# A planned order of steps, reckoned with shorter landings of loads and searched anew

## The chip, the cores and the metric

One core of one Trainium2 chip runs the whole program. The metric is the device time of one execution in microseconds (us); a kernel's time is the median of its runs. TensorE is called PE here, VectorE DVE, ScalarE ACT, GpSimd POOL; SP is the queue that issues nearly all DMAs.

## The reference

Three layers follow one another, all in float32: an attention over 32 pooled memory slots (4 batches, 8 heads, 576 tokens, 64 wide), a gated layer and a layer with a leaky ReLU, both over the 2304 x 512 result.

```python
a = softmax(phi, axis=2)                       # over the 576 tokens, 32 slots
k_m = einsum('bhsm,bhsd->bhmd', a, k)          # pooled keys; v_m the same with v
attn = softmax(q @ k_m^T / 8) @ v_m
x = attn.transpose(0, 2, 1, 3).reshape(2304, 512)
x = ((x @ w_a) * (x @ w_b)) @ w_out            # 512 -> 1536 -> 512
h = x @ w_in                                   # 512 -> 2048
out = maximum(0.01 * h, h) @ w_out2            # 2048 -> 512
```

## The kernel before

The work has two stages. The first (up to 382 us of the profile) holds the attention, the gated layer and the preparation of the weights of the last layer; the second is the last layer, whose loops are written out by hand and which the change doesn't touch.

In the first stage nothing is ordered by hand. Functions such as `plan_att`, `plan_wab`, `plan_wo`, `plan_w`, `plan_ab`, `plan_x1` and `plan_pair` hand steps to a planner, the class `Plan` at the head of the file. A step has an engine, a cost in us, the steps that it needs, a due time, and a function that emits its instructions. `Plan.run` plays the engines forward in time: each engine takes, among the steps that could start first, the one with the smallest `latest`. `Plan.order` first sets `latest` from the due times and a few passes back and forth, then shifts it with `shifts`: each number in `SEEDS` draws one window of the plan and moves some of the steps in it by up to 12 us either way. The result is one order of steps for each engine's queue, and each queue is worked off in that order on the chip. So the planner's clock has no direct effect there: only the order that it leads to, and the number of filling matmuls, counts.

The filling matmuls (`warm`, line 1680) are products of constants that go into PE's queue wherever the planner reckons PE to be idle, as long as its clock is below `WARM` = 27.0 us. They are 512 or 256 columns wide and compute nothing that is used.

Loads and stores go through one queue in the planner. Each takes its own cost (0.85 us for a half of `phi`, 2.0 and 1.05 for the two parts of the first `k`, 2.5 and 1.05 for those of the first `v`, 1.5 for a half of `q`, 1.46 for a 512 KB weight block), from 0.8 us on. A load's data is reckoned to be there at the end of its cost plus a lag `late`. The lag begins at `LATE[0]` = 4.0. It is raised by `FETCHED` at the first load that is put in behind 9.0 us, raised again by `FETCHED`, up to `LATEST`, whenever PE's instructions enter a new block of 256 behind 20 us while the DMA queue is busy, and set to `LATE[1]` = 2.3 when the queue has stood idle for over 1 us:

```python
# lines 207-208, in issue(); lines 297-300, in run()
if free[DMA] + 2.0 > entered > 20.0:
    late[0] = min(late[0] + self.FETCHED, self.LATEST)
...
if at > free[DMA] + 1.0:
    late[0] = self.LATE[1]
elif free[DMA] > 9.0 and late[0] == self.LATE[0]:
    late[0] += self.FETCHED
```

The start of the plan matters for what follows. The first twelve loads have a fixed rank: the halves of `phi`, `k` and `q` of batch 0, the first two weight blocks (`wab` 0, of `w_a` and `w_b`), the two parts of `v`, two more weight blocks. A weight block is widened by three steps: the high words on ACT (line 438), the low words on POOL (line 446) or ACT (line 442), and their joining on DVE (line 456). From `v` a chain goes through PE, ACT and DVE: pooling (`km`, line 771), division (`kc`, line 844), transposition (`kvT`, line 858), the product with the weight block (`wp`, line 1183), its parts on ACT and DVE (`W`, lines 1208 and 1212). A second chain goes from `q` through the scores to the softmax on DVE (the last division is line 1100), the transposition of its result (`aT`, line 1110) and its parts (`AT`, lines 1123 and 1127). Both meet in the first `ab` product (line 1246), which needs `W` and `AT`. From there on the planner has real work for PE at all times: `ab`, the products with `w_out` (`x1p`, line 1312), the attention of batches 1 to 3, and the further `wp`.

Of the kernel before, what the change touches and what calls it, by code (L numbers as in the profile page):

```python
# [46 lines left out]
class Plan:  # L47
# [10 lines left out]
    BLOCK, FETCH, FETCH_ALONE, START = 256, 6.9, 4.8, 50.0  # L58
    CHANGE = 12
    SWITCH = {"rf": 0.1, "tf": 0.1, "fr": 0.28, "ft": 0.22, "rs": 0.1, "ts": 0.1, "sr": 0.3, "st": 0.23, "fs": 0.2, "sf": 0.2}  # L60
    LATE, FETCHED, LATEST = (4.0, 2.3), 1.2, 5.2
    SEEDS = (683652, 560159, 530175, 125177, 433488, 159828, 165231, 686446, 405802, 158260, 349165, 253408, 67255,
# [4 lines left out]
    PASSES, URGENT, WASTE = 30, 1.0, 0.3  # L67

    def __init__(self, **pools):
# [25 lines left out]
    def order(self, idle=None):  # L95
# [16 lines left out]
        for x, l in zip(self.steps, latest):  # L112
            x.latest = l
        for seed in self.SEEDS:
            for i, d in self.shifts(seed, best[2]):
# [1909 lines left out]
```

## Time and profile before

| What | us |
|---|---|
| Median of 3 runs (lowest to highest) | 738.47 (737.46 to 738.53) |
| The profiled execution | 738.45 |
| Its span, first to last instruction | 736.4 |
| PE busy / DVE busy / ACT busy in the span | 729.4 / 579.1 / 413.7 |
| Granted TensorE clock | 1.00 in the whole span |

The profile is of one execution. A row of a timeline begins with the start and the length of a piece in us; the engine, the line and the tiles that are written and read follow, with the number of instructions and, in brackets, the idle time of the engine before it and what ended that. The chain of work is followed back from the last instruction, at each step to what released it.

### The profile page before, as it was taken

The numbers are of one execution on the slowest core, as the hardware profiler recorded it, in microseconds if no ns is written. First come the engines' busy times: TensorE is split into PE (matmuls) and PEld (weight loads), VectorE is DVE, ScalarE is ACT, GpSimd is POOL, SyncE is SP. The second block draws the span as 40 slices with busy tenths as digits, with TensorE's granted clock in tenths as the row PEclk, the third lists the DMA queues.
The fourth block names the chain that finished last, engine by engine and source line by source line (L and its number), as shares of the span: only waits on it lengthen the run. The fifth ranks groups of instructions, "written<-read, shape, count | busy, mean of one in ns | idle before, by whom it ended". The sixth has DMA issues, their size and how long they took to land.

```text
span 736.4 us, 14535 instructions
## 1 busy us (share of the span) xinstructions
PE 729.4 (99%) x5391; PEld 654.2 (89%) x5391; DVE 579.1 (79%) x1196; ACT 413.7 (56%) x915; POOL 20.1 (3%) x38
## 2 busy tenths in 40 slices
PE   8999999999999999999999999999999999999997
PEld 5787887988889798888899999999999999999987
DVE  5987786967809999998746767998866997877797
ACT  3886684866729787856414455644444743454442
POOL 1210000001300000000000000000000000000000
PEclk9999999999999999999999999999999999999999
DMA  9995267474605989876527877778987777997493
GB/s 312 359 395 184 77 219 246 158 241 131 218 3 199 319 311 320 296 239 250 206 93 253 263 252 250 254 256 256 295 286 258 261 245 249 288 289 246 152 304 88
DMA packets 87495, 175.27 MB, mean 238 GB/s; under 512 B 7553, under 2 KB 36737, under 8 KB 87425
## 3 DMA queue, kind: packets, MB, share of 16 engines
q1 hardware_dynamic: 86736, 173.77, 70.6%
q8 instruction: 42, 0.69, 0.4%
q10 hardware_dynamic: 688, 0.59, 0.3%
q14 instruction: 29, 0.23, 0.1%
HBM read 140.25 MB, written 34.08 MB: 237 GB/s over the span
## 4 chain that ended last, share of the span: by engine, by line
PE 93%; DVE 3%; DMA 2%; ACT 1%; issue 0%; SPq 0%; DVEq 0%
PE h L1750 24%; PE x1p L1312 19%; PE ab L1246 19%; PE o L1850 15%; PE o L1854 8%; PE wp L1183 3%; DMA stage<-in_moe_w_b_dram 1%; PE sc L1050 1%; PE qT L1014 1%; PE km L758 1%; PE km L771 1%; PE aT L1110 1%; PE warm L1680 1%; DMA phi_t<-in_phi_dram 1%; DVE w2o L1434 0%; PE h L1825 0%
## 5 line engine op out<-in xcount | busy, mean ns | idle before, releaser
L1850 PE MATMUL o<-w2o,S 128*128 128x512 f32 (+1 forms) x504 | 177.1, 386 | 0.0
L1246 PEld LDWEIGHTS ab<-AT,W 128*128 128x128 f32 x1152 | 154.8, 188 | 7.0 <-ACT W L1208 2.5
L1246 PE MATMUL ab<-AT,W 128*128 128x288 f32 x1152 | 160.0, 297 | 0.2
L1312 PE MATMUL x1p<-G,wo 128*128 128x512 f32 (+1 forms) x720 | 156.5, 372 | 0.0
L1802 ACT ACTIVATE S<-g 128x384 fp32r<-128x384 f32 x168 | 87.6, 523 | 99.2 <-PE o L1850 85.9
L1312 PEld LDWEIGHTS x1p<-G,wo 128*128 128x128 f32 x720 | 123.5, 189 | 22.2 <-issue 0.8
L1750 PE MATMUL h<-T,ring 128*128 128x384 f32 x720 | 141.8, 335 | 0.0
L1854 PE MATMUL o<-w2o,S 128*128 128x256 f32 x492 | 137.6, 280 | 0.0
L1750 PEld LDWEIGHTS h<-T,ring 128*128 128x128 f32 x720 | 120.9, 188 | 4.1
L1803 DVE TENSOR_TENSOR S<-g,S 128x384 fp32r<-128x384 f32 x168 | 91.5, 553 | 40.4 <-ACT S L1802 40.2
L1850 PEld LDWEIGHTS o<-w2o,S 128*128 128x128 f32 x504 | 93.7, 188 | 14.5
L1854 PEld LDWEIGHTS o<-w2o,S 128*128 128x128 f32 x492 | 92.8, 189 | 0.0
L1872 DVE TENSOR_TENSOR C<-C,o 128x768 f32<-128x768 f32 x75 | 71.0, 949 | 13.9 <-ACT C L1876 7.9
L1750 PE MATMUL h<-B,ring 128*128 128x384 f32 x288 | 57.2, 336 | 0.0
L1793 DVE TENSOR_TENSOR g<-g 128x384 f32<-128x384 f32 x96 | 52.3, 552 | 2.9 <-ACT g L1760 2.4
L1750 PEld LDWEIGHTS h<-B,ring 128*128 128x128 f32 x288 | 48.8, 188 | 1.6
L438 ACT ACTIVATE stage<-stage 128x512 f32<-128x512 f32 x68 | 46.0, 686 | 5.6 <-DMA stage<-in_moe_w_in_dram 2.5
L1268 DVE TENSOR_TENSOR g<-a_sb,ab 128x288 f32<-128x288 f32 x96 | 42.1, 446 | 5.8 <-PE ab L1246 4.8
L1263 ACT COPY a_sb<-ab 128x288 f32<-128x288 f32 x96 | 38.3, 402 | 12.9 <-PE ab L1246 12.5
L1283 ACT ACTIVATE G<-g 128x576 fp32r<-128x576 f32 x48 | 33.2, 691 | 12.6 <-DVE g L1268 12.5
L1212 DVE TENSOR_TENSOR W<-wp,W 128x256 fp32r<-128x256 f32 (+1 forms) x75 | 35.1, 491 | 5.5 <-ACT W L1208 4.7
L1208 ACT ACTIVATE W<-wp 128x256 fp32r<-128x256 f32 (+1 forms) x75 | 30.3, 449 | 15.9 <-PE wp L1183 8.4
(143 smaller groups left out, 737.5 us busy)
## 6 DMA issues: line engine op xcount, KB each, us to landing
w2o<-a_scr SPq DMA_DIRECT2D x168, 256.0 KB, 3.8
ring<-a_scr SPq DMA_DIRECT2D x72, 512.0 KB, 4.4
stage<-in_moe_w_out_dram SPq DMA_DIRECT2D x28, 512.0 KB, 5.2
a_scr<-w2o SPq DMA_DIRECT2D x24, 512.0 KB, 3.7
a_scr<-a_out SPq DMA_DIRECT2D x24, 512.0 KB, 4.1
stage<-in_moe_w_in_dram SPq DMA_DIRECT2D x16, 512.0 KB, 5.2
stage<-in_moe_w_a_dram SPq DMA_DIRECT2D x12, 512.0 KB, 8.4
stage<-in_moe_w_b_dram SPq DMA_DIRECT2D x12, 512.0 KB, 7.5
```

The costliest lines, as they stand in the source:

```text
L438: act.activation(out=x, in_=x, func=ACTF.Prelu, scale=2.0 ** -112, alpha=2.0 ** 32)
L1246: pe.matmul(out=c[x, n][:, :HS], lhsT=W[b, f][:, hw, g, 128 * x:128 * x + 128], rhs=AT[b][:, g, ha, n * HS:(n + 1) * HS], start=(g == 0 an ...
L1263: act.copy(c["sb"][:, n], c[0, n][:, :HS])
L1268: dve.tensor_tensor(out=c["g"][:, n], in0=c["sb"][:, n], in1=c[1, n][:, :HS], op=ALU.mult)
L1312: pe.matmul(out=c["ps"], lhsT=wo_t[f][:, hw, 128 * m:128 * m + 128], rhs=G[f][:, hg, first:first + n], start=(f == fs[0] and (hw, hg) == P ...
L1750: pe.matmul(out=out, lhsT=ring[i % 2, part][:, o, kp, hw], rhs=x[:, hx], start=fresh and kp == 0 and (hw, hx) == PASSES[0], stop=kp == 1 a ...
L1793: dve.tensor_tensor(out=t, in0=x, in1=y, op=op)
L1802: act.activation(out=t[:, 0], in_=src, func=ACTF.Copy)
L1803: dve.tensor_tensor(out=t[:, 1], in0=src, in1=t[:, 0].bitcast(F32), op=ALU.subtract)
L1850: pe.matmul(out=dst[:, u, :y - x], lhsT=hi, rhs=wide[:, x:y], start=fresh and x == 0, stop=False, skip_group_check=True,)
L1854: pe.matmul(out=dst[:, u, :256], lhsT=lo, rhs=t[:, 0], start=False, stop=q == 3, skip_group_check=True,)
L1872: o_adds.append(lambda x=x: dve.tensor_tensor(out=total[name], in0=total[name], in1=x, op=ALU.add))
```

## The change

Two of the planner's constants are changed. The lag of a load is raised by 0.4 us instead of 1.2 us at a time, and to 4.8 us at most instead of 5.2. The list of seeds is a new one, of 105 numbers where there were 53. No step, cost or due time is different, so the same instructions run on the chip but for the number of filling matmuls; their order in the queues of the first stage is another one.

```diff
-    LATE, FETCHED, LATEST = (4.0, 2.3), 1.2, 5.2
-    SEEDS = (683652, 560159, 530175, 125177, 433488, 159828, 165231, 686446, 405802, 158260, 349165, 253408, 67255,
...
+    LATE, FETCHED, LATEST = (4.0, 2.3), 0.4, 4.8
+    SEEDS = (735747, 237875, 338390, 284576, 668393, 453202, 159564, 193473, 1221, 69595, 734897, 407191, 651114,
...
```

## Rows read from the trace of the kernel before

**Rows 1.** Stretches of the span: length, busy time of each engine, granted clock, DMA share, GB/s
```profile
0.00:27.09 27.09, 24.41 (x328) 16.26 (x328) 18.67 (x42) 11.75 (x24) 5.49 (x19) 1.00 0.99 324
27.09:60.00 32.91, 32.87 (x372) 28.39 (x365) 29.67 (x55) 28.33 (x55) 4.85 (x6) 1.00 0.95 346
60.00:382.33 322.33, 321.80 (x2662) 279.58 (x2661) 247.39 (x571) 210.02 (x502) 9.73 (x13) 1.00 0.61 210
382.33:736.40 354.07, 350.31 (x2041) 329.95 (x2039) 283.35 (x531) 163.59 (x336) 0.00 (x0) 1.00 0.77 247
```

**Rows 2.** Groups by line, PE up to 27.09 us: the filling matmuls
```profile
L1680 PE MATMUL warm<-const-float32-1.0 128*128 128x256 f32 (+1 forms) x22 | 10.0, 570 | 0.8 <-PEq L2009 0.8
```

**Rows 3.** Chain of work, 10 to 30 us: start, length, piece
```profile
18.72 0.09 PE sc L1056 x4
18.81 1.49 PE warm L1680 x4
20.30 2.17 PE km L771 x72
...
24.32 0.59 PE wp L1183 x16
24.92 1.13 PE aT L1110 x9
...
26.50 0.67 PE wp L1183 x16
27.17 3.13 PE ab L1246 x19
```

**Rows 4.** Timeline of SP, the tenth and the fifteenth load
```profile
8.06 2.24 SPq L570 DMA_DIRECT2D kv_t<-in_v_dram  x1
17.47 1.14 SPq L431 DMA_DIRECT2D stage<-in_moe_w_b_dram  x1
```

**Rows 5.** DMA issues, the same two: KB, us from issue to landing
```profile
kv_t<-in_v_dram SPq DMA_DIRECT2D x1, 384.0 KB, 10.5
stage<-in_moe_w_b_dram SPq DMA_DIRECT2D x1, 512.0 KB, 8.6
```

**Rows 6.** Timeline of ACT, the step behind the pooling of v
```profile
22.50 0.62 ACT L844 ACTIVATE kc<-km,r 128x128 f32<-128x128 f32 x2 [1.31 <-PE km L771]
```

**Rows 7.** Timeline of DVE, around the last division of the first softmax
```profile
23.38 0.76 DVE L1100 TENSOR_TENSOR s<-s,m 128x576 f32<-128x576 f32 x1
24.06 0.68 DVE L456 SCALAR_TENSOR_TENSOR wab<-stage 128x512 int32<-128x512 int32 x1
25.42 0.42 DVE L1212 TENSOR_TENSOR W<-wp,W 128x256 fp32r<-128x256 f32 x1 [0.68 <-ACT W L1208]
25.76 0.68 DVE L456 SCALAR_TENSOR_TENSOR wab<-stage 128x512 int32<-128x512 int32 x1
```

**Rows 8.** Stretch of 10 us, columns as in rows 1
```profile
40.00:50.00 10.00, 9.96 (x79) 8.23 (x78) 8.67 (x15) 8.08 (x18) 1.18 (x1) 1.00 1.05 396
```

**Rows 9.** Who waited for whom, PE from 27 to 345 us: us, times, longest
```profile
PE aT L1110 <- DVE s L1100: 0.2, 1, 0.2
PE kvT L926 <- ACT kmn L917: 0.2, 1, 0.2
```

**Rows 10.** Chain of work over the span: an early and a late run of ab
```profile
27.17 5.40 PE ab L1246 x36
...
338.04 19.32 PE ab L1246 x144
```

**Rows 11.** Timeline of SP, the first of five loads issued in a row
```profile
176.08 0.37 SPq L431 DMA_DIRECT2D stage<-in_moe_w_b_dram  x1
```

**Rows 12.** Chain of work, 176 to 196 us
```profile
178.49 8.90 DMA stage<-in_moe_w_b_dram
...
187.41 0.70 ACT stage L438
188.11 0.29 ACT a_sb L1263
```

12 rows, old and new, of the table SEEDS are left out of this document.

## The prediction

> **What bounds the kernel now.** I read the stretches of the span first [rows 1]. PE is busy for 32.87 of 32.91 us from 27.09 to 60, for 321.80 of 322.33 in the rest of the first stage, and for 350.31 of 354.07 in the second, whose code the change doesn't touch. So PE's queue sets the time, and an order of steps can win in three places only: in the first 27.09 us, in the 0.6 us of idle time of the first stage behind them, and in what is lost between matmuls that count as busy.
>
> In the first 27.09 us PE is busy for 24.41 us, but 10.0 of these are the 22 filling matmuls [rows 1, 2]. That is waiting under another name. What ends it is read from the chain of work [rows 3]: scores of batch 0 up to 18.81, then four fillers of 1.49 us, the pooling of `v` at 20.30, `wp` at 24.32, `aT` at 24.92, a second `wp`, and at 27.17 the first `ab`. PE works its queue off in order, so the pooling could not begin before the fillers ahead of it were through, even if its data was there.
>
> It was there. The second part of `v` was issued at 8.06 and landed 10.5 us later, at 18.56 [rows 4, 5]. The planner's own clock, summed from its costs, has that load's end at 0.8 + 2 x 0.85 + 2.0 + 1.05 + 2 x 1.5 + 2 x 1.46 + 2.5 + 1.05 = 15.02 us, and with the lag of 5.2 its data at 20.22. So the lag measured is 18.56 - 15.02 = 3.5 us, and the fillers stand where the planner believed the data to be still away. The fifteenth load tells the same: its end is five weight blocks later, at 22.32; it landed at 17.47 + 8.6 = 26.07, a lag of 3.75 [rows 4, 5].
>
> **The change part by part.** (1) The lag of the early loads. By the code the raise comes with the eighth load, the first that is put in behind 9.0 us. From there the reckoned lag falls from 5.2 to 4.4, and to 4.8 once PE's instructions have entered a new block behind 20 us, against 3.5 to 3.75 measured. The new figure is nearer to the chip and still on the safe side of it, by 0.7 to 1.3 us: no early step gets into a queue ahead of data that is later than reckoned.
>
> `v` is reckoned to be there 0.8 us earlier, at 19.42 in place of 20.22. Worth: of the 1.49 us of fillers about 0.8 go, and the pooling begins about 0.8 earlier. The most is 1.49, all of the fillers [rows 3]. What follows must move too. ACT, next in the chain, had been idle for 1.31 us waiting for the pooling, so it can take the division 0.8 earlier [rows 6]. The first `wp` moves from 24.32 to about 23.5. The softmax chain comes in beside it: its last division ends on DVE at 23.38 + 0.76 = 24.14, and `aT` began at 24.92 because PE was in `wp` (24.32 + 0.59) [rows 3, 7]. With `wp` through by 24.1, `aT` can begin at 24.15, 0.77 earlier. Both chains thus move by about the same, and the first `ab` by 0.75 to 0.8, to about 26.4. DVE has room for it: 0.68 us idle at 25.42, and two joins of 0.68 at 24.06 and 25.76 of which at least the second can stand behind the parts of `AT` [rows 7]. That makes 0.68 + 0.68 = 1.36 us, the most that this start can give. The least is 0, if the search leaves DVE in another order in which the softmax ends later. I take 0.8, the row of the fillers cut by the change of the reckoning.
>
> (2) The stretch from 27.09 to 60 us. A PE that is 0.8 us ahead asks for its weights 0.8 us earlier, and the loads can't come earlier: the DMA engines stand at a share of 1.05 in the ten us behind 40 [rows 8]. What hides that is the earliness just measured, 1.5 us for the fifteenth load (26.07 against 27.52). PE's idle time in this stretch is 0.04 us [rows 1], so no load was on its path. Cost 0; if the cover is gone, the whole 0.8 is given back.
>
> (3) The lag behind 60 us. Behind a gap in the queue it starts at 2.3 before and after, but is then raised by 0.4 and not 1.2. Here the reckoning was not too long. Five weight blocks were issued from 176.08 on; the fifth, issued at 178.49, landed 8.90 us later at 187.39 [rows 11, 12]. One gap lag of 2.3 and five costs of 1.46 from 176.08 give 185.7, so the chip was 1.7 us later. ACT took that block's high words at 187.41, at the moment of landing, and the copy `a_sb` stood behind them until 188.11, with `ab` waiting for it in the chain [rows 12]. Shorter raises put more such conversions too early into ACT's queue, ahead of copies that PE needs. What PE loses to all waits from 27 to 345 us now is 0.2 + 0.2 us of idle time [rows 9], and some gaps hidden in busy time. I take 0; from below -0.4 (both idle times gone), from above +0.6 (three more of 0.2).
>
> (4) The new seeds. They put the attention of batches 1 to 3 and the weight work at other places between the same matmuls. What can be had or lost is seen in `ab`: the first 36 of a run take 5.40 / 36 = 150 ns each, 144 in a late run 19.32 / 144 = 134 ns [rows 10], so 36 x 16 ns = 0.58 us went in waits that no idle time shows. A new order may take that away or bring it at another place: 0, from -0.6 to +0.6.
>
> The sum is -0.8 + 0 + 0 + 0, against the profiled execution of 738.45, which lies 0.02 us under the median: 737.65, say **737.6 us**. Single bounds add up to -1.36 - 0.4 - 0.6 = -2.4 and 0 + 0.6 + 0.6 = +1.2; together from 736.1 to 739.7.
>
> **The rivals.** *A larger gain.* The search also finds the rest of the start, 1.36, and about half of parts (3) and (4), 0.5: 736.6. For it speaks that PE has 10.0 us of fillers at the start; against it that DVE has only 1.36 us to give.
>
> *Nothing comes of it*, which is also the case in which the reckoning's 0.8 doesn't reach the chip: the loads from 27 to 60 us set the pace, PE gains 0.8 at the start and waits 0.8 behind it, at `ab` or `x1p`: 738.4. For it speaks the DMA share of 1.05 [rows 8]; against it the 0.04 us of idle time and the 1.5 us of earliness. [...]
>
> *Slower.* Of part (3): after 60 us conversions are queued on ACT ahead of loads that land later than reckoned, and PE stops for lack of `W` or free `ab` banks. The lag is shorter by up to 0.8 us after one raise, so a stop costs up to 0.8. The start's gain is used up at one such stop; four of them make 738.45 - 0.8 + 3.2 = 740.9. For it speaks the load that landed 1.7 us behind the reckoning; against it that this cost PE no idle time that the waits show, because PE itself was late too.
>
> **How the numbers follow.** About what a measurement can tell from no change is 0.2%, 1.48 us here: under 736.97 is faster, over 739.93 slower. Forecast 0.50, larger gain 0.25, nothing 0.17, slower 0.08. The larger gain lies mostly beyond the bound: 0.21 of it, and 0.03 of the forecast, make faster 0.24. Of slower 0.06 lies beyond. The same is 0.70. The range reaches to the larger gain and past the case of nothing, 736.2 to 739.1; it leaves out the ends of the bounds added up and stops of more than one.
>
> **What would show it.** Right: fewer fillers between the scores and the pooling of `v`, that pooling near 19.5, the first `ab` near 26.4, and `h`, the first product of the second stage, earlier by the same. Wrong in part (1): the pooling earlier but `ab` still near 27.1, with DVE without idle time before it. Wrong in part (2): idle time of PE from 27 to 60 us that a load or a join ended. Wrong in part (3): new idle time or slower `ab` runs behind 60 us, with ACT on line 438 at the moment of a landing just ahead. Wrong in all: a second stage that doesn't take the same time.

## The result and the profile after

The changed kernel takes 741.92 us (median of 5 runs, 740.85 to 743.55) against 738.47 for the kernel before in the same comparison: a ratio of 1.0051, with a 95% interval of 1.0036 to 1.0066. It is slower by about half a per cent, and the prediction of 737.6 (736.2 to 739.1) was wrong, in the sign too.

The profiled execution took 740.85 us, its span is 738.8. Line numbers are higher by 4 than before. Stretches of the span with the same four borders as in [rows 1], that is the first `ab`, 60 us, and the first `h` (columns as there):

```profile
0.00:26.07 26.07, 24.58 (x326) 16.02 (x327) 18.34 (x42) 12.54 (x26) 4.86 (x18) 1.00 0.97 318
26.07:60.00 33.93, 33.63 (x370) 29.13 (x368) 31.82 (x57) 27.78 (x54) 5.41 (x7) 1.00 0.96 350
60.00:384.70 324.70, 322.76 (x2658) 279.34 (x2658) 243.71 (x567) 213.33 (x506) 5.29 (x7) 1.00 0.60 208
384.70:738.80 354.10, 350.37 (x2041) 329.96 (x2039) 283.44 (x531) 163.58 (x336) 0.00 (x0) 1.00 0.77 247
```

The first `ab` comes at 26.07 and not at 27.09: 1.02 us were gained at the start. The second stage is the same, 354.10 against 354.07. Between them lie 33.93 + 324.70 = 358.63 us against 32.91 + 322.33 = 355.24: 3.39 us more. The sum -1.02 + 3.39 + 0.03 is the 2.4 us by which the span grew. PE's idle time (length less PE's busy time) in these two stretches grew from 0.57 to 2.24 us, which makes 1.67 of the 3.39; the rest, 1.7, is time that counts as busy.

The start in the chain of work of the kernel after (answers [rows 3]):

```profile
18.16 0.09 PE sc L1060 x4
18.25 1.06 PE warm L1684 x2
19.31 2.17 PE km L775 x72
```

The fillers between scores and the pooling of `v` took 1.06 us and not 1.49, and the pooling began at 19.31 and not at 20.30. Of these 0.99 us the fillers are thus 0.43; the other 0.56 come from the scores, which ended at 18.25 and not at 18.81.

Who waited for whom, PE from 26.07 to 384.7 us of the kernel after (us in total, times, longest; answers [rows 9]):

```profile
PE kvT L930 <- issue: 1.2, 1, 1.2
PE ab L1250 <- DVE g L1272: 0.4, 1, 0.4
PE wp L1187 <- DVE wab L460: 0.3, 1, 0.3
```

Three single waits, and the largest is one that the kernel before doesn't have at all: "issue", time in which PE waited for nothing that the profile shows. Timeline of PE around it, kernel after (start, length, piece, idle time before it):

```profile
154.04 2.25 PE L762 MATMUL km<-kv_t,phi_t 64*32 64x128 f32 x144
156.22 0.38 PE L898 MATMUL km<-ones,es 128*128 128x2 f32 x2
156.47 1.63 PE L1316 MATMUL x1p<-G,wo 128*128 128x512 f32 x6
159.32 0.43 PE L930 MATMUL kvT<-ident,kmn 128*128 128x128 f32 x2 [1.22 <-issue]
```

The pooling of batch 3 on line 762 sends 144 matmuls and 144 weight loads through PE in 2.25 us, six matmuls of `x1p` follow, and then PE stands still for 1.22 us ahead of `kvT`. The weight load of this `kvT` had been done at 158.17; only its matmul didn't come.

What did PE wait for? Packets of 16384 bytes on DMA queue 8, of the kind "instruction", number 42 in the span, against 10778 matmuls and weight loads of PE: one for 257 on average. Counting PE's instructions in blocks of 256, the planner's own figure, with the same offset in every kernel, PE enters block 12 at 154.32, inside that pooling, and block 13 at 159.32, the moment at which it goes on; 257 of the recorded ones start in between. The DMA queues in two windows in between, kernel after (packets, MB, share of 16 engines):

```profile
q1 hardware_dynamic: 618, 0.83, 99.8%
...
q1 hardware_dynamic: 109, 0.39, 97.0%
q8 instruction: 1, 0.02, 6.1%
```

The first line is 154.32 to 156.94, the other two are 156.94 to 157.93. For 2.62 us after the block was entered the DMA engines carried nothing but stores and loads; then came the one instruction packet, 1 us long, and 1.4 us later PE went on. In the kernel before the same block is entered at 150.97, the DMA engines carry a single packet of 3.0% up to 151.61, and PE's packet starts at 151.62: no pause. The pooling and the first `kvT` there, timeline of PE, kernel before:

```profile
150.58 2.25 PE L758 MATMUL km<-kv_t,phi_t 64*32 64x128 f32 x144
...
155.47 0.33 PE L926 MATMUL kvT<-ident,kmn 128*128 128x128 f32 x1 [0.17 <-ACT kmn L917]
```

### The profile page after: what moved, and what is told of

Same layout as the page of the kernel before. It is cut to its first block, busy times and chain, and to the rows that moved or that the text cites. A ratio compares the mean times of both kernels' runs of the same rounds, so it can differ in the third digit from the quotient of the medians.

```text
span 738.8 us, 14487 instructions
## 1 busy us (share of the span) xinstructions
PE 731.3 (99%) x5389; PEld 654.5 (89%) x5389; DVE 577.3 (78%) x1196; ACT 417.2 (56%) x921; POOL 15.6 (2%) x32
## 4 chain that ended last, share of the span: by engine, by line
PE 94%; DVE 3%; ACT 2%; issue 1%; DVEq 0%; ACTq 0%
PE h L1754 24%; PE ab L1250 19%; PE x1p L1316 19%; PE o L1854 15%; PE o L1858 8%; PE wp L1187 3%; PE warm L1684 1%; PE sc L1054 1%; PE qT L1018 1%; PE km L762 1%; PE km L775 1%; PE aT L1114 0%; ACT W L1212 0%; ACT stage L442 0%; PE h L1829 0%
## 5 line engine op out<-in xcount | busy, mean ns | idle before, releaser
L1291 DVE TENSOR_TENSOR G<-g,G 128x576 fp32r<-128x576 f32 x48 | 36.1, 752 | 3.3 <-ACT G L1287 2.5
```

## The experiments

**The same kernels again.** The changed kernel once more, and the kernel before once more.

> The changed kernel unaltered, looked at a second time. Its five timed runs lie between 740.85 and 743.55 us, those of before between 737.46 and 738.73, so something in it differs from execution to execution. Theory A (a fixed loss of the order): the same places lose time as in its first profile, first of all PE idle for 1.2 us ahead of a kvT matmul near 158 us, and the time is 740.9 to 742. Theory B (the landings of the early loads decide, since the order leaves them no room): the first ab product is later than the 26.07 us of the first profile by as much as the loads ahead of it landed later, and the rest of the spread is there, in the first 60 us.

> The kernel before, unaltered, looked at a second time. In its first profile the second part of v landed at 18.60 us; in the profiles of four other kernels with the same first ten loads it landed at 19.0 to 20.2. If the landing differs from execution to execution: it is later here, up to 20.2, and the pooling of v and the first ab stay at 20.3 and 27.1 all the same, because the fillers stand ahead of them.

After: 742.62 us, ratio 1.0055 (1.0036 to 1.0074); first `ab` at 26.92, 359.22 us from there to `h`, the pause at the same `kvT`, 1.4 us. Before: first `ab` at 27.95, 354.93 to `h`. So the loss between `ab` and `h` repeats (3.4 to 4.3), and so does the pause. The start doesn't stand where it stood: it moved by 0.85 us in both kernels with the landings of the loads, and the expectation that it stays at 27.1 was a miss. The difference at the start, 1.03 here, repeats.

**The start alone.** The kernel before without the fillers between scores and the pooling of `v`, then without all up to `wp` (23.0 in place of 19.2):

```diff
-        return sorted(self.trial(idle, seen)[0], key=lambda x: x.start)
+        own = set(self.steps)
+        out = self.trial(idle, seen)[0]
+        out = [x for x in out if x in own or not 17.0 < x.start < 19.2]
+        return sorted(out, key=lambda x: x.start)
```

> The order of the kernel before, without the one 512-wide and the one 256-wide filling matmul between the scores and the pooling of v (1.49 us in the chain of before); nothing else differs. It does part (1) of the prediction alone. If the start's gain is real and is carried to the end: pooling of v near 19 us instead of 20.3, first ab 0.7 to 1.0 us earlier than 27.1, time 737.5 to 737.9. If it is given back (loads, DVE): ab earlier but the second stage begins where it did, 738.4. If DVE holds the first ab: ab still at 27.1.

> The kernel before without any filling matmul that the plan has between 17 and 23 us, those between scores and pooling and those between pooling, kvT and wp. Leaving out the first group alone moved the first ab by 0.8 to 1.0 and the median by nothing. Theory (the start is worth what it moves, but is given back in part where the loads from 27 to 60 us set the pace): first ab 25.9 to 26.4, time 737.6 to 738.5 against about 738.5 to 739.4 of before on the same chip, ratio 0.998 to 1.000. Rival (the fillers hold the granted clock up): clock under 1.0 somewhere in the first 40 us, and slower by over 1 us.

First `ab` at 26.27 and 26.34, 354.9 and 355.7 us from there to `h`; 738.50 and 738.66 us, ratios 0.9999 (0.9989 to 1.0008) and 0.9999 (0.9990 to 1.0007). The profiled start moves as the prediction's part (1) says, and the median shows nothing of it: the 737.5 to 737.9 that was expected of the first didn't come, though a gain of up to 0.8 us stays within the interval. Without these fillers too the mean granted clock was 0.999 and 1.000. With the fillers up to `wp` gone, the softmax holds PE instead, and some of the gain is lost right behind the start (0.4 us by 46 us). No version tried here beats the kernel before.

**Is the pause the instruction stream?** The changed kernel with other work in front of the first pooling, so that every later instruction of PE stands elsewhere in its blocks: 54 tiny matmuls added (216 instructions), fillers cut narrower (112 more), or three fillers replaced by 57 tiny matmuls (216 more).

```diff
             step.emit()
+            if step not in own and 2.0 < step.start < 3.0:
+                for _ in range(54):
+                    pe.matmul(
+                        out=warm_ps[:32, :16], lhsT=unit[:64, :32], rhs=unit[:64, :16], start=True, stop=True
+                    )
```

> The changed kernel with 54 tiny filling matmuls (216 PE instructions) put in at the start, while PE waits for the first phi. Modulo 256 that moves every place in PE's instruction stream by 40 against the blocks in which it is fetched. Theory A (the 1.2 us ahead of kvT near 158 us is a wait for the next block of PE's instructions, which the pooling's 288 instructions had used up too fast): that idle time is gone or at another instruction, the time 0.8 to 1.4 us under the changed kernel's. Rival (a semaphore, ACT or a DMA holds that kvT): the idle time is there at the same instruction, the time the same.

> The changed kernel with its filling matmuls cut narrower at equal total width (the first three into 6 of 88 columns, the other 512-wide ones into 4 of 128, the 256-wide ones into 2 of 128): 112 more PE instructions ahead of the first ab, no more time. If the wait of 1.4 to 1.5 us ahead of kvT near 158 us is for the next block of PE's instructions: it goes, as it went with 216 instructions, and here nothing is paid at the start, so the time is 1.2 to 1.6 us under the changed kernel's 742.3, at 740.7 to 741.1. If the wait only moves to another instruction: 742.3.

> The changed kernel with its first three 512-wide filling matmuls (they end before 6 us) replaced by 57 tiny ones of about the same time in all. So every later instruction of PE stands 216 places further back in its stream, and no step, wait or order is different. Theory (the 1.4 us near 158 us are PE waiting for its next block of 256 instructions, because a block is entered during the pooling of batch 3, whose 288 instructions pass in 2.2 us): the pause at the line of kvT behind that pooling goes, first ab stays near 26.1 to 26.9, from the first ab to h about 356.7 in place of 358.5 to 359.2, and the time is 740.3 to 741.2, some 1.4 to 1.8 under the changed kernel. Rival (the pause comes from the order: ACT's kmn or a queue of PE that waits for a tile): it stays at 1.2 to 1.4, and the time stays at 741.9 to 742.6. A mixed outcome: the pause goes and another one comes at another block's edge, with the same sum.

The pause is gone in all three. All three were expected to be faster than the changed kernel; they took 744.74, 744.22 and 743.33 us and were slower, since the first `ab` came at 30.84, 29.91 and 29.50. The narrow matmuls took longer than reckoned (the 57 of the third 6.23 us, where the fillers that they replace take 5.13), and what followed them was slower too (in the first kernel the two 256-wide fillers behind them took 1.06 us and not the 0.60 of the changed kernel, and the mean granted clock of the span was 0.998 against 1.000; in the third, four fillers that take 1.92 us in the chain of the changed kernel took 3.08). From `ab` to `h` the three took 356.74, 357.79 and 358.28 us. From the first `ab` to `h` there are the same matmuls in the same order in these kernels, so they can be laid on each other: at the `kvT` of the pause the three gain 1.28 us on the kernel after, but the next matmul takes 0.13 of it back, and in the third kernel an `aT` that now waits for DVE another 0.17. Net, the pause costs about 1.1 us. The hope of 356.7 held for the first only; the others lose again at single `ab` matmuls elsewhere (0.65 us ahead of the one at 196.78 in the second, 0.3 ahead of the one at 271.44 in the third).

**Does the fetch wait behind the loads?** The changed kernel with the load of `w_a` that is issued at 152.86 put behind the two stores that follow it; PE's stream is unchanged.

```diff
-        return sorted(self.trial(idle, seen)[0], key=lambda x: x.start)
+        out = self.trial(idle, seen)[0]
+        moved = [x for x in out if x.engine == DMA and 153.0 < x.start < 154.0]
...
+        return sorted(out, key=lambda x: 157.0 if x in moved else x.start)
```

> The changed kernel with one load moved in SP's queue: the block of w_a issued at 152.86 is put behind the two stores that follow it, to about 157; PE's stream is the same, so the block edge is at the same instruction in the pooling of batch 3. Theory (the fetch of the block waits behind the data transfers that are in flight when it is asked for): with one load of 512 KB less in flight the fetch's packets start 0.6 to 1.6 us behind the edge and not 2.6, and the pause of 1.2 to 1.4 us at kvT goes or shrinks to under 0.6; from the first ab to h 357.0 to 357.8. Rival (the delay of the fetch is PE's own and has nothing to do with the load): the pause stays at 1.2 to 1.4, from the first ab to h 358.5 to 359.2. In both cases the moved block lands some 4 us later, and if its conversion stands ahead of a copy on ACT, a wait of up to 1 us can come near 165.

PE enters block 12 at 155.89, inside the same pooling; the DMA engines are nearly empty, the packet starts 0.77 us later, and there is no pause. DMA queues from the entry to the packet's start, and over the packet (155.89 to 156.65, 156.65 to 157.78):

```profile
q1 hardware_dynamic: 35, 0.08, 26.2%
...
q1 hardware_dynamic: 31, 0.13, 27.8%
q8 instruction: 1, 0.02, 6.2%
```

Timeline of PE of this kernel, the rows that answer those of the pause:

```profile
155.61 2.25 PE L765 MATMUL km<-kv_t,phi_t 64*32 64x128 f32 x144
157.79 0.38 PE L901 MATMUL km<-ones,es 128*128 128x2 f32 x2
158.04 1.63 PE L1319 MATMUL x1p<-G,wo 128*128 128x512 f32 x6
159.60 0.59 PE L933 MATMUL kvT<-ident,kmn 128*128 128x128 f32 x2
```

With the DMA engines 26.2% busy behind the entry the packet came 0.77 us after it, with 99.8% it came 2.62 after: in these two runs it was the transfers in flight that held up the fetch. The time is 741.73 us, ratio 1.0050 (1.0032 to 1.0069): the gain doesn't show. The 358.06 us from `ab` to `h`, a little above the 357.0 to 357.8 expected, are only 0.4 less than in the first profile of the kernel after and 1.2 less than in the second; `v` landed late in this profile, and two `ab` near 43 us lose 0.3. What is left, 3.0 us over the kernel before, is not this pause.

**Lag or search?** The orders without any seeds, with the first half of each list, and with two lists of four made-up seeds, each under the old and the new lag (shown for seeds 11 to 44 under the new lag, against the kernel before). The old list under the new lag, or the new list under the old, leads the planner to a point at which no step can start; these two crossings have no order.

```diff
-    LATE, FETCHED, LATEST = (4.0, 2.3), 1.2, 5.2
-    SEEDS = (683652, 560159, 530175, 125177, 433488, 159828, 165231, 686446, 405802, 158260, 349165, 253408, 67255,
...
+    LATE, FETCHED, LATEST = (4.0, 2.3), 0.4, 4.8
+    SEEDS = (11, 22, 33, 44,)
```

> The order without any seeds, reckoned with the old lag (1.2, 5.2). It separates the reckoning from the search. As a base for the next run; slower than before by 2 to 5 us, since the search is left out.

> The order without any seeds, reckoned with the new lag (0.4, 4.8). If the shorter lag itself is worth what the prediction said: 0.5 to 1 us faster than the same with the old lag. If the shorter lag itself costs (orders that trust loads too early): slower than it by 1 us or more. If both are alike, the loss of the changed kernel lies in the seeds, that is in the order the search ended with.

> Old lag with only the first 26 of the kernel before's 53 seeds, an order from half way through its search. Theory A (any order other than the one before's searched one loses on the chip, and the lag doesn't matter): from the first ab to h 356 to 358, above before's 354.9 to 355.1. Theory B (it is the shorter lag that makes orders worse): 355.0 to 356.0, and no pause of PE for its instructions of over 0.5 us.

> New lag with only the first 52 of the new 105 seeds. Theory A (the order, not the lag): from the first ab to h 356 to 360, like the order with half of the old seeds but for one pause of 1.4 us at most. Theory B (the shorter lag): at 358 to 362, at least 2 us over its pair with the old lag, with the pause for instructions in the pooling of batch 3 or other waits behind loads.

> Old lag with four made-up seeds (11, 22, 33, 44), an order that nothing was searched for. Theory A (order, not lag): from the first ab to h anywhere from 356 to 360, in the same spread as the new lag's orders. Theory B (lag): 356 to 357, with no pause for instructions, as the order without seeds has it (356.7).

> New lag with the same four made-up seeds. Theory A (order, not lag): from the first ab to h 356 to 360, and the pause for instructions only by chance of where the block's edge falls. Theory B (lag): over 358, at least 2 us over its pair with the old lag; the order without seeds had 366.1 here.

> Old lag with four other made-up seeds (555, 666, 777, 888). Theory A (order, not lag): from the first ab to h in the same spread as with the new lag, 356 to 360. Theory B (lag): 356 to 357, without a pause for instructions.

> New lag with the same four other made-up seeds. Theory A (order, not lag): from the first ab to h 356 to 360, within 1 us of its pair either way but for the pause for instructions. Theory B (lag): at least 2 us over its pair.

From the profiles (us); "stop" is PE's wait on "issue" behind the pooling of batch 3, "a_sb" its waits for that copy. "By the plan" is the same stretch on the planner's own clock, from the start of the first `ab` to the end of PE's last step. It needs no chip: it is what the planner in each kernel's code reckons, and the pooling of batch 3 stands at the same place in PE's queue in plan and trace, in all ten.

| Seeds | lag | first `ab` | `ab` to `h` | by the plan | stop | a_sb | median, ratio |
|---|---|---|---|---|---|---|---|
| own list | old | 27.09 | 355.1 | 353.0 | 0 | 0 | 738.47 |
| own list | new | 26.07 | 358.5 | 354.2 | 1.2 | 0 | 741.92, 1.0051 |
| half | old | 27.69 | 357.6 | 355.8 | 0.2 | 0 | 741.01, 1.0027 |
| half | new | 26.71 | 363.3 | 358.2 | 1.3 | 0 | 747.03, 1.0105 |
| none | old | 27.33 | 356.7 | 355.6 | 0 | 0 | 741.16, 1.0021 |
| none | new | 26.46 | 366.1 | 357.9 | 2.6 | 1.5 | 747.67, 1.0109 |
| 11 to 44 | old | 27.38 | 357.8 | 356.2 | 0 | 0.2 | 741.93, 1.0033 |
| 11 to 44 | new | 26.08 | 365.4 | 359.4 | 2.6 | 2.9 | 747.58, 1.0112 |
| 555 to 888 | old | 28.15 | 362.9 | 361.7 | 0.6 | 0 | 746.84, 1.0093 |
| 555 to 888 | new | 26.70 | 376.8 | 368.3 | 3.5 | 3.4 | 760.09, 1.0276 |

In five pairs of five the new lag brings the first `ab` 0.9 to 1.5 us earlier and loses 3.4 to 13.8 us between `ab` and `h`. In the first two pairs the lists differ too; in the last three the lag alone does. The theory that any other order loses as much, whatever the lag, has fallen; the shorter lag as such makes the orders worse on the chip. Orders differ too: under the old lag from 355.1 to 362.9. There the theory of the lag asked for 355 to 357 and missed three times (357.6, 357.8, and 362.9 with a stop of 0.6). What it asked of the pairs, at least 2 us more with the new lag, came each time. The order without seeds was 1.7 us slower than the kernel before and not 2 to 5. The two searches: under the old lag the searched order is 1.6 us better than the one without seeds, under the new lag 7.7 better. The new search had a worse start to make good, and made good most of it.

The loss has two parts. The first stands in the plans themselves: with the shorter lag the planner's own order is 1.2 to 6.6 us longer on its own clock, on which every load lands just as reckoned. So this part isn't loads that land too late; it is a worse order, and why a planner that is told of earlier loads finds a worse one stays open. The second is what the chip adds to the plan: 1.1 to 2.1 us under the old lag, 4.3 to 8.5 under the new. The stop belongs there, and in the three new orders that weren't searched it cost more than its length, by an estimate, since the granted clock was lower behind it: 0.53 from 160.5 to 167 us without seeds and 0.74 from 160.4 to 167 with seeds 11 to 44; with 555 to 888 it was 0.91 on average from 140 to 180 us, where the stop lies. PE was busy for 6.50 of 6.50 and 6.53 of 6.60 us of the first two stretches, so by an estimate from these rows the lower clock cost another 6.5 x 0.47 = 3.1 and 6.6 x 0.26 = 1.7 us there, and in the third order 40 x 0.09 = 3.6 us at most, the stop's own share included.

PE's waits show best in an order that nothing was searched for. Who waited for whom, PE behind 24 us, seeds 11 to 44 with the new lag:

```profile
PE ab L1242 <- ACT a_sb L1259: 2.9, 4, 1.7
PE km L890 <- issue: 2.6, 1, 2.6
PE aT L1106 <- DVE AT L1123: 0.3, 1, 0.3
```

The same with the old lag:

```profile
PE qT L1010 <- ACT kmn L913: 0.7, 1, 0.7
PE ab L1242 <- ACT a_sb L1259: 0.2, 1, 0.2
```

The wait of 1.7 us, on the timeline of ACT of the new one (start, length, piece, idle time before it and what ended it):

```profile
33.62 0.68 ACT L434 ACTIVATE stage<-stage 128x512 f32<-128x512 f32 x1 [0.36 <-DMA stage<-in_moe_w_a_dram]
34.21 0.67 ACT L1279 ACTIVATE G<-g 128x576 fp32r<-128x576 f32 x1
35.16 0.68 ACT L438 ACTIVATE stage<-stage 128x512 int32<-128x512 uint32 x1 [0.28 <-DMA stage<-in_moe_w_b_dram]
35.74 0.65 ACT L434 ACTIVATE stage<-stage 128x512 f32<-128x512 f32 x1
36.29 0.57 ACT L1204 ACTIVATE W<-wp 128x512 fp32r<-128x512 f32 x1
36.77 0.68 ACT L1259 COPY a_sb<-ab 128x288 f32<-128x288 f32 x2
```

ACT stands idle twice, each time until a weight block lands, and works off the blocks' conversions, 0.65 to 0.68 us each; the copy `a_sb` that PE's `ab` needs stands behind them in the queue. The two idle times, 0.36 + 0.28 = 0.64 us, are what loads later than reckoned cost here. Most of the wait is in the plan already: in it ACT works through the same pieces without a pause, two conversions and a `W` stand ahead of the copy, and PE is reckoned idle for 0.93 us ahead of this `ab`.

**What the lag really is.** On the planner's clock the first part of `v` has its end at 15.02 - 1.05 = 13.97. Issue on SP's timeline (the first of the two issues starts the row) and time to landing, kernel after:

```profile
7.03 3.92 SPq L574 DMA_DIRECT2D kv_t<-in_v_dram  x2
...
kv_t<-in_v_dram SPq DMA_DIRECT2D x1, 768.0 KB, 11.0
```

The same in the kernel with half of the new seeds, with its timeline of PE:

```profile
6.58 4.31 SPq L566 DMA_DIRECT2D kv_t<-in_v_dram  x2
...
kv_t<-in_v_dram SPq DMA_DIRECT2D x1, 768.0 KB, 12.9
...
18.05 1.13 PE L1676 MATMUL warm<-const-float32-1.0 128*128 128x512 f32 x2
19.55 2.20 PE L767 MATMUL km<-kv_t,e 64*64 64x128 f32 x72 [0.37 <-DMA kv_t<-in_v_dram]
```

It landed at 18.03 in the one, a lag of 4.1, and at 19.48 in the other, a lag of 5.5: later than the new figure of 4.4 and than the old of 5.2, and there PE stood idle for it. For the second part of `v`, on which the prediction rests, the lag was 3.6 us in the kernel before's first profile and 3.6 to 6.4 in the eighteen profiles of this study; 10 of the 18 lie above 4.4, 6 above 4.8, 4 above 5.2. Most of this spread isn't of `v` alone. The first part of the first `k` landed between 8.04 and 9.63 us, and in 14 of the 18 the second part of `v` came 10.4 to 10.6 us behind it; in the other four it came 11.4 to 12.1 behind it. PE's first pooling reads that `k`, so a late `k` makes PE late as well: in the second profile of the kernel before `v` landed 1.5 us later, and the first `ab` came 0.9 later.

## Why the prediction was wrong

**The step that failed: parts (3) and (4), the 0 behind 60 us.** The prediction took 0 for what the shorter lag and the new seeds do there, with at most +0.6 each; about +2.9 was measured. It comes from a pause of PE for its instructions (1.1), one full DVE queue (0.6) and about 1.2 in many small gaps, all told below. The gain of the start was real and about as large as forecast; this stretch is what set the time.

**Part (1), the start: right in direction, its size in part by luck.** Fewer fillers, the pooling near 19.5 (19.31), the first `ab` near 26.4 (26.07): -0.8 expected, -1.02 measured, and -0.9 to -1.5 in the five pairs. But of the 0.99 by which the pooling moved only 0.43 were fillers, where 0.8 had been reckoned; 0.56 came from scores that ended earlier, which the prediction doesn't name. Of its signs all came but the last: `h` is 2.4 us later and not earlier.

**Part (1), the safety: untrue, and its price not shown.** "The new figure is nearer to the chip and still on the safe side of it" took the lag from one execution, 3.5 to 3.75 us [rows 4, 5], and that execution was one of the two earliest of eighteen. The old figure of 5.2 covers 14 of the 18, the new one of 4.4, by which `v` is planned, 8. What looked like waste in one profile was in part a margin for others. That this margin is what the changed kernel lost isn't shown: much of the spread moves PE too, the start kept its gain in both profiles, and PE's waits for `a_sb` in the changed kernel are 0 and 0.2 us.

**Part (2), 27 to 60 us: perhaps mis-sized a little.** Cost 0 expected; PE's idle time there rose from 0.04 to 0.30 us, ended by a join on DVE (`wp` <- `wab` 0.3 above), and two of the three shifted kernels, whose `ab` begins 4.8 and 3.8 us later and whose loads are thus earlier against PE, are 0.5 us better by 46 us, the third (3.4 later) isn't. So up to half a microsecond may have been given back: the rival *nothing comes of it* in part.

**Why the 0 was wrong.** Three reasons. The prediction summed the planner's clock for the loads, but not to the end: there the changed plan ends its first stage at 379.9 us and the one before at 379.1, with the first `ab` 0.5 earlier and the way from it 1.2 longer. So the plan itself said that the new order was no gain. Then, the bounds came from the waits left in the kernel before [rows 9, 10]. That order was the result of a search, so the waits that a search removes were no longer to be seen in its trace; orders under the same lag that were not searched lose 1.6 to 7.9 us between `ab` and `h`. And the largest single loss, the pause for instructions, has no row there at all: 1.22 us idle, 1.1 net. What follows in size is one full DVE queue at 348 us, which the plan doesn't have either. Chain of work, kernel after, the end of a row of DVE pieces that begins at 335:

```profile
346.62 0.67 DVE G L1291
347.28 0.09 DVE T L1589
347.37 0.17 issue
347.54 0.46 DVE g L1272
347.99 0.04 issue
348.04 5.05 PE ab L1250 x36
```

The step `g` that frees an `ab` bank stands behind sums for the last layer's weights (`T`, line 1589), and `ab` loses 0.6 us there. It does so in every kernel with this order. The rest, about 1.2 us, is spread. By the two traces, between the starts of matmuls of one kind, from `ab` to `h`, 63 steps are 60 to 130 ns longer than their kind's median, 5.7 us in all, against 55 and 4.9 us before, and the 124 changes from one kind of matmul to another take 23.8 us without the idle time, against 22.8 us for 121 before; in part these figures hold the two losses above too. No single place carries the rest, and what makes each of them wasn't settled. The 1.2 us by which the plan grew are of the same kind (0.8 of PE idle, 0.4 of changes) and the same size; they weren't matched place by place.

**The rivals.** *Slower* had the right sign and was about a microsecond short (740.9). Its mechanism, conversions ahead of loads that land later than reckoned, is seen in the unsearched orders (a_sb, 1.5 to 3.4 us), though part of these waits was in the plan, as at the one of 1.7 us above; in the changed kernel the search had cleared them. What it hadn't cleared is when PE's instructions arrive. The planner does reckon with them: behind 50 us it holds a block back until 4.8 us after PE has entered the one before (`FETCH_ALONE`). On the chip it came 5.0 us after (154.32 to 159.32), so the figure was near. The place was off: the planner counts this edge some 37 instructions later than the trace shows it, at the scores that follow, and so reckons the block to be there 1.9 us before it is needed.

Why a shorter lag leads to the pause is shown in part. In all ten orders the edge falls inside this pooling, so its place is not the difference. In all five with the new lag the DMA engines are over 97% busy from the entry into the block until the fetch starts, 2.4 to 3.2 us later; with the old lag that takes 0.6 to 1.7 us in four and 3.1 in the fifth (555 to 888, with a stop of 0.6). That loads are issued earlier because buffers are reckoned free earlier is a reading and wasn't tried by itself. *A larger gain* found nothing for it.

## What to carry to other kernels

Before a planner's figure is changed, let the planner's own clock run to its end with the new one: here it already had the way from `ab` to `h` 1.2 us longer, and in four other pairs 2.2 to 6.6. A margin in a plan is to be judged by the spread of many executions, not by the slack in one profile, which was one of the two earliest of eighteen here. Bounds on what a new order can lose don't come from the waits of a searched order, which has had its waits removed; one order without the search, run once, shows what lies behind them. And a stretch with many short instructions on an engine should not fall together with a full DMA queue: 288 instructions of PE in 2.25 us, with the DMA engines over 97% busy, were followed here by stops of 1.2 to 3.5 us.

## What the runs showed of the hardware

- **PE's instructions came over the DMA engines, beside the data.** They came in packets of 16384 bytes, 42 for 10778 recorded instructions; in the changed kernel the one from 156.94 to 157.93 took 6.1% of the 16 engines' time, loads and stores 97.0%. At this pooling the fetch began 0.65 and 0.77 us after the block was entered where the engines were 3.0% and 26.2% busy up to it, and 2.4 to 3.2 us after in the six profiles with the new lag's order left as it was, where loads and stores kept them 97.7 to 103.0% busy. PE went on 1.4 us after the packet's end in the changed kernel, and 5.0 us after it had entered the block before (4.7 with seeds 11 to 44 under the new lag, 155.79 to 160.47). The pooling's 288 instructions had passed in 2.25 us, and PE stood still for 1.2 to 3.5 us in these six.
- **Behind three pauses of 2.6 to 3.5 us the granted clock was lower.** They are those of the three unsearched orders with the new lag. In the order without seeds and with the new lag, PE stood still for 2.6 us. Stretches of that kernel (columns as in [rows 1]):

```profile
150.00:157.00 7.00, 7.00 (x159) 5.72 (x161) 5.96 (x17) 5.21 (x13) 0.00 (x0) 1.00 0.47 181
157.00:160.50 3.50, 0.92 (x37) 0.65 (x18) 0.00 (x0) 0.00 (x0) 0.00 (x0) 0.90 0.97 308
160.50:167.00 6.50, 6.50 (x22) 5.33 (x23) 0.33 (x2) 3.25 (x9) 0.65 (x1) 0.53 0.99 324
167.00:174.00 7.00, 7.00 (x112) 5.08 (x111) 3.87 (x11) 3.94 (x9) 1.32 (x2) 1.00 0.03 9
```

  The granted clock was 1.00 before the pause, 0.90 in the 3.5 us around it and 0.53 in the 6.5 us behind it, then 1.00 again. With seeds 11 to 44 and the new lag, at 0.74, six matmuls of `x1p` took 2.18 us behind the pause, and 1.63 in the changed kernel at 1.00. Around the changed kernel's pause of 1.2 us it was 1.00 (140 to 180 us).
- **The tiny matmuls took 72 and 109 ns a product.** 54 products of 16 columns, two matmuls in each, took 3.9 us in the first shifted kernel (4.46 to 8.33), 72 ns each; 57 at the very start of the third took 6.23 us, 109 ns each. The first pooling moved by more, from 9.2 in the changed kernel to 14.0 in the first: the next four fillers (two 512 and two 256 wide) took 1.68 and 1.06 us there, and the mean granted clock of its span was 0.998.
